# Head transposes in the last quarter of an expert's results, and a count of 48 ahead of two lists

## The chip, the cores and the metric

The kernel runs on one core of a Trainium2 chip. The metric is device time in microseconds (us), the median of several executions. A profiled execution is recorded beside them, with its own time. TensorE, the matmul engine, is called PE here; VectorE is DVE, ScalarE ACT, GpSimd POOL, and SyncE's DMA queue SP.

## What is computed

Three layers in a row on 2304 tokens (4 batches of 576, 8 heads of 64): an attention with a memory read, a feed-forward layer, and a mixture of eight experts. The edit lies in the third:

```python
logits = x @ w_gate
flat = logits.flatten()
order = np.argsort(-flat)
assigned = -np.ones(N, dtype=np.int64)
counts = np.zeros(E, dtype=np.int64)
for idx in order:
    tok, e = (int(idx) // E, int(idx) % E)
    if assigned[tok] >= 0 or counts[e] >= cap:
        continue
    assigned[tok] = e
    counts[e] += 1
...
for e in range(E):
    mask = assigned == e
    h = np.maximum(x[mask] @ w1[e], 0.0)
    out[mask] = h @ w2[e]
```

Here N = 2304, E = 8, cap = 288, the model width is 512 and the hidden width 1024. All values are float32.

## The kernel before

Each float32 operand of a large product is split into a high part (a copy on ACT, rounded to fp32r) and a low part (a subtraction on DVE or POOL); one product is three matmuls of the parts.

**Routing** (class `Moe`, generator `routes`). The assignment is made in phases. A phase finds the next expert that fills up: a search in two rounds of three steps (`search`), in which DVE compares (`cmp`), PE counts with 18 small products (line 727), DVE compares the counts with the room left (`fl`), and PE spreads the answer with one small product (line 732). Then come a count (line 779) and a prefix (lines 832 and 833). Behind it stand the expert's number, its four weight loads of 1 MB on SP (`load`), their conversion on ACT and POOL (`convert`, tiles `wraw` to `wsp`), and the list of its tokens (`lists`): DVE makes one-hot rows `oh` in two halves, PE multiplies them with 18 small products (line 870), DVE writes the indices `idx`, and POOL gathers 3 x 96 token rows into `xg` (`gather`, line 933). A list is made in small pieces beside the next expert's search: `spare` advances it where the search leaves room. `self.wants` says what the next piece needs: "v" DVE, "p" PE.

**Experts** (generator `mlps`). For each expert in the order found: 8 hidden blocks of 12 products (`hidden`, 288 columns each), then 4 result blocks of 24 products (`output`), each of 128 of the 512 result columns. The tokens of an expert come in by 12 transposes of `xg` into the PSUM tile `tr`, which has two buffers, and four splits into `xs` (`head`, pairs of k = 0, 1 and 2, 3). The results go out by 12 transposes (`tail`) in the next expert's hidden blocks 1 to 3, a copy on ACT and an indirect DMA on POOL.

**Order.** The order on PE is the program's: `mlps` yields after every product or transpose, and `run` counts these steps. The generator `routes` yields how many steps shall pass before its next small products are written; these numbers stand in `GAPS`, and GAPS[8] stands ahead of a list's product that no search accompanies:

```python
            for _ in self.mlps(routes):
                wait -= 1
                if wait <= 0 and len(self.ready) <= self.done + AHEAD:
                    wait = next(routes, NEVER)
```

While no list is ready, at the start, `run` takes the numbers only for a test (10 or more: write one piece of other work). A planner with a cost model of its own orders the instructions of DVE, ACT, POOL and SP within what the dependences allow. Weights are converted into six buffers, four for one expert; POOL runs its conversions, gathers and result transfers from one queue.

Before the change `mlps` wrote the first pair of the next expert's transposes ahead of result block 2, and the second pair ahead of block 3. In `routes`, list 6 (the last but one) was finished without any yield ahead of its product, and lists 0 and 7 with GAPS[8] = 36.

Of the kernel before, what the change touches and what calls it, by code (L numbers as in the profile page):

```python
# [359 lines left out]
KD = DM // 128  # L360
# [200 lines left out]
NE = 8  # L561
# [3 lines left out]
KE = FE // 128  # L565
# [5 lines left out]
CUTS = (2, 2, 2, 2)  # L571
ON_DVE = ()
LEAD = 12
HEAD_AT = 2
GAPS = (60, 12, 12, 15, 12, 12, 12, 18, 36, 6)
AHEAD = 3


class Moe:
# [127 lines left out]
    def search(self, val, hot, gaps, unit, beside=None):  # L707
# [3 lines left out]
        for s in range(3):  # L711
# [18 lines left out]
            pj = self.p1.tile([128, NE], F32, name="rs")  # L730
            yield GAPS[9]
            nc.tensor.matmul(pj, self.jones[unit][s][0:r], fl[0:r], start=True, stop=True)
# [9 lines left out]
    def phase(self):  # L742
# [24 lines left out]

        b = yield from self.search(hi, hot, GAPS[0:3], 0, lower)

        V.scalar_tensor_tensor(lw, hi, b, lof, op0=OP.subtract, op1=OP.add)  # L770
        b = yield from self.search(lw, hot, GAPS[3:6], 1)
        for s, op in enumerate((OP.is_gt, OP.is_equal)):
# [4 lines left out]
        ps = self.p1.tile([128, 2 * NTT * NE], F32, name="rs")  # L777
        yield GAPS[6]
        nc.tensor.matmul(ps, self.ones, gm.rearrange("p t e -> p (t e)"), start=True, stop=True)
# [47 lines left out]
    def prefix(self, ab):  # L827

        nc, V = self.nc, self.nc.vector
        pf = self.p1.tile([128, 2, 2, NTT], F32, name="rs")  # L830
        yield GAPS[7]
        nc.tensor.matmul(pf[:, 1], self.ones, ab[:, :, 0:NTT], start=True, stop=True)
# [50 lines left out]
    def routes(self):  # L883

        self.beside = self.wants = None
        for i in range(NE):
            if i < NE - 1:
                yield from self.phase()
            else:
                while self.wants is not None:  # L890
                    self.spare(self.wants)
                yield from self.rest()
            er = self.number()
            if i == 0:
                self.settle()
            self.split[i] = self.convert(self.load(er))
            self.beside = self.lists(i)
            self.wants = next(self.beside)
            if i in (0, NE - 1):
                while self.wants is not None:  # L900
                    if self.wants == "p":
                        yield GAPS[8]
                    self.spare(self.wants)

    def load(self, er):
        nc, raws = self.nc, []
# [86 lines left out]
    def mlps(self, routes):  # L993

        yield from self.head(0, range(KD))
        for i in range(NE):
            for f in range(KE):
                yield from self.hidden(i, f)
                if 1 <= f <= 3 and i:
                    yield from self.tail(i - 1, [f - 1])  # L1000
            for d in range(KD):
                if d >= HEAD_AT and i + 1 < NE and d < HEAD_AT + 2:
                    while len(self.ready) <= i + 1:
                        next(routes, None)
                    yield from self.head(i + 1, [2 * (d - HEAD_AT), 2 * (d - HEAD_AT) + 1])
                yield from self.output(i, d)
            self.done = i + 1
        yield from self.tail(NE - 1, range(3))

    def run(self, other, settle):  # L1010

        self.settle = settle
        with self.tc.manual_schedule(engines={mybir.EngineType.PE}):
            routes, wait = self.routes(), 0
            while not self.ready:
                if next(routes, 0) >= SLOW:
                    next(other, None)
            for _ in range(LEAD):
                wait = next(routes)
# [4 lines that stand above are left out]
# [106 lines left out]
```

## Time and profile before

| what | value |
|---|---|
| median of 3 runs (lowest to highest) | 1120.62 us (1119.87 to 1121.05) |
| profiled execution | 1114.29 us |
| its span, first to last instruction | 1112.6 us |
| what lies around the span | 1.69 us |
| mean granted TensorE clock | 0.933 |
| PE busy | 987.1 us (89%) |
| DVE, ACT, POOL busy | 663.3, 572.5, 533.9 us |

The profile is one execution, with times counted from the span's start. [...] The time in square brackets behind a row is the engine's idle time just before it, and what ended it. The expert stage starts near 796 us and PE's last product ends near 1105 us.

### The profile page before, as it was taken

To read this page: it belongs to the slowest core of one execution; us is meant where nothing else is said; L and a number is where in the kernel's file an instruction comes from. 1 tells how busy PE (TensorE), PEld (TensorE's weight loads), DVE (VectorE), ACT (ScalarE), POOL (GpSimd) and SP (SyncE) were. 2 spreads that over 40 slices of the span, in tenths; PEclk is the share of its full clock that TensorE was granted. 3 is DMA by queue.
4 is the path that set the end of the run, shared out by engine and by line. 5 is a ranking of instruction groups with operands and counts; after the bars stand their busy time and mean duration, and the time that the engine had idled before them with its cause. 6 is when DMAs were issued, how large, how long until landed. Compare 5 with 4: busy or idle time off the path is not lost.

```text
span 1112.6 us, 21194 instructions
## 1 busy us (share of the span) xinstructions
PE 987.1 (89%) x7561; PEld 907.2 (82%) x7561; DVE 663.3 (60%) x2012; ACT 572.5 (51%) x1471; POOL 533.9 (48%) x550
## 2 busy tenths in 40 slices
PE   4777799999999988999999999995679899969997
PEld 3555578888888978899999999983569888869996
DVE  7999887878788547783223232337756467653120
ACT  6877787978787645553223343421343244334531
POOL 3765656655566436553221112110772675575751
PEclk9877899999999999999999999995599899998998
DMA  6455435463444487475552323102453255425510
GB/s 147 113 138 135 124 109 167 103 176 92 141 97 132 135 294 249 131 232 197 202 162 95 114 86 102 52 19 55 161 174 135 60 195 172 137 83 192 174 37 29
DMA packets 135499, 148.74 MB, mean 134 GB/s; under 512 B 69857, under 2 KB 102625, under 8 KB 132321
## 3 DMA queue, kind: packets, MB, share of 16 engines
q1 hardware_dynamic: 132320, 137.94, 40.6%
q0 software_dynamic: 3072, 9.44, 2.8%
q8 instruction: 60, 0.98, 0.4%
q14 instruction: 47, 0.38, 0.1%
HBM read 109.60 MB, written 37.75 MB: 132 GB/s over the span
## 4 chain that ended last, share of the span: by engine, by line
PE 49%; DVE 21%; DMA 9%; issue 8%; ACT 7%; POOL 4%; SPq 1%; another core or an unknown queue 1%; POOLq 0%; DVEq 0%; ACTq 0%
PE ph L942 11%; PE ph L43 5%; PE ph L44 5%; PE ph L45 5%; PE py L43 3%; PE py L44 3%; PE py L45 3%; DMA raw<-in_moe_w_in_dram 3%; POOL wsp L925 2%; PE ps L308 2%; DMA wraw<-in_moe_w_dram 2%; PE rs L727 2%; PE ps L213 2%; DMA raw<-in_moe_w_out_dram 2%; DVE P L224 2%
## 5 line engine op out<-in xcount | busy, mean ns | idle before, releaser
L447 POOL TENSOR_TENSOR gf<-r 128x288 f32<-128x288 f32 x128 | 90.7, 709 | 239.2 <-ACT r L445 230.3
L925 POOL TENSOR_TENSOR wsp<-wraw,wsp 128x1024 fp32r<-128x1024 f32 x64 | 150.5, 2383 | 48.1 <-ACT wsp L923 45.4
L26 DVE TENSOR_TENSOR gs<-gf,gs 128x288 fp32r<-128x288 f32 x128 | 64.7, 506 | 106.5 <-ACT gs L25 106.1
L942 PE MATMUL ph<-xs,wsp 128*128 128x288 f32 x768 | 122.4, 310 | 0.0
L942 PE MATMUL ph<-hs,wsp 128*128 128x288 f32 x768 | 121.0, 313 | 0.0
L942 PEld LDWEIGHTS ph<-xs,wsp 128*128 128x128 f32 x768 | 109.1, 196 | 5.0 <-issue 4.3
L942 PEld LDWEIGHTS ph<-hs,wsp 128*128 128x128 f32 x768 | 110.6, 200 | 2.2 <-issue 1.4
L242 POOL TENSOR_SCALAR P<-P,R,og 128x128 f32<-128x128 f32 (+2 forms) x144 | 98.9, 703 | 23.2 <-DVE pta L26 9.6
L44 PE MATMUL py<-gs,wout 128*128 128x288 f32 x320 | 94.6, 298 | 0.9 <-DVE gs L26 0.8
L43 PE MATMUL ph<-xt,win 128*128 128x288 f32 x320 | 95.1, 297 | 0.1
L45 PE MATMUL ph<-xt,win 128*128 128x288 f32 x320 | 94.9, 297 | 0.0
L44 PE MATMUL ph<-xt,win 128*128 128x288 f32 x320 | 94.8, 296 | 0.0
L43 PE MATMUL py<-gs,wout 128*128 128x288 f32 x320 | 92.3, 298 | 1.6 <-ACT gs L25 1.1
L923 ACT ACTIVATE wsp<-wraw 128x1024 fp32r<-128x1024 f32 x64 | 63.9, 1050 | 57.7 <-DMA wraw<-in_moe_w_dram 36.8
L45 PE MATMUL py<-gs,wout 128*128 128x288 f32 x320 | 93.6, 296 | 0.0
L445 ACT ACTIVATE r<-ph 128x288 f32<-128x288 f32 x128 | 52.0, 406 | 76.6 <-PE ph L45 76.0
L236 ACT ACTIVATE P<-P,R 128x128 f32<-128x128 f32 (+2 forms) x144 | 83.4, 580 | 11.3 <-DVE R L224 10.8
L25 ACT ACTIVATE gs<-gf 128x288 fp32r<-128x288 f32 x128 | 56.5, 441 | 56.3 <-POOL gf L447 53.2
L213 PE MATMUL ps<-kt,qt 64*128 64x128 f32 (+3 forms) x384 | 58.7, 385 | 16.8 <-DVE ptb L26 9.1
L267 PE MATMUL ps<-ident,P 128*128 128x128 f32 x320 | 61.9, 302 | 11.5 <-DVE R L224 3.6
L43 PE MATMUL ph<-xs,win 128*128 128x288 f32 x192 | 62.8, 327 | 3.2 <-ACT yo L478 1.9
L26 DVE TENSOR_TENSOR ptb<-ps,ptb 128x384 fp32r<-128x384 f32 (+3 forms) x128 | 59.4, 466 | 8.8 <-ACT ptb L25 7.0
(227 smaller groups left out, 2683.8 us busy)
## 6 DMA issues: line engine op xcount, KB each, us to landing
wraw<-in_moe_w_dram SPq DMA_DIRECT2D x32, 1024.0 KB, 7.6
xt<-xs_d SPq DMA_DIRECT2D x16, 1152.0 KB, 5.7
x_d<-xo SPq DMA_DIRECT2D x32, 288.0 KB, 3.6
xf<-x_d SPq DMA_DIRECT2D x32, 288.0 KB, 3.5
xs_d<-xs SPq DMA_DIRECT2D x8, 1152.0 KB, 5.3
y<-yp_d SPq DMA_DIRECT2D x16, 576.0 KB, 5.4
raw<-in_moe_w_in_dram SPq DMA_DIRECT2D x32, 256.0 KB, 3.2
raw<-in_moe_w_out_dram SPq DMA_DIRECT2D x32, 256.0 KB, 2.9
```

Of the source, the lines that this page charges most:

```text
L26: (eng or nc.vector).tensor_tensor(lo, src, hi.bitcast(F32), op=OP.subtract)
L43: nc.tensor.matmul(out, lhi, rhi, start=start, stop=False)
L44: nc.tensor.matmul(out, lhi, rlo, start=False, stop=False)
L45: nc.tensor.matmul(out, llo, rhi, start=False, stop=stop)
L213: nc.tensor.matmul(ps[j][:, 0:w], qt[r0, a, qs], kt[r0, b, 0:w], start=i == 0, stop=i == 2)
L236: nc.scalar.activation(pw, pw, AF.Exp, bias=R[:, 0, u:u + 1], scale=-1.0, accum_out=R[:, 1, u:u + 1])
L242: nc.gpsimd.tensor_scalar(PP[n][w], PP[n][w], R[:, 2, w:w + 1], og9[:, hp, w:w + 1], op0=OP.mult, op1=OP.mult)
L267: nc.tensor.transpose(tr[:, 128 * i:128 * i + 128], P[:, 128 * i:128 * i + 128], ident)
L447: nc.gpsimd.tensor_tensor(gf, r, r, op=OP.mult)
L923: nc.scalar.activation(w[:, 0, hs], raw[:, hs], AF.Copy)
L925: eng.tensor_tensor(w[:, 1, hs], raw[:, hs], w[:, 0, hs].bitcast(F32), op=OP.subtract)
L942: nc.tensor.matmul(out, l[a], r[b], start=i + p == 0, stop=i == n - 1 and p == 2)
```

## The change

The first edit is in `mlps`. The next expert's transposes no longer stand ahead of result blocks 2 and 3. The blocks 0 to 2 are written whole; then come the first pair (k = 0 and 1), 12 products of block 3, the second pair (k = 2 and 3), and the other 12 products. The second is in `routes` and GAPS: finishing a list becomes a method, `finish`, which yields GAPS[8] ahead of the list's product. It is now used for list 6 as well, and GAPS[8] is 48 instead of 36.

```diff
-HEAD_AT = 2
-GAPS = (60, 12, 12, 15, 12, 12, 12, 18, 36, 6)
+GAPS = (60, 12, 12, 15, 12, 12, 12, 18, 48, 6)
...
             if i < NE - 1:
                 yield from self.phase()
             else:
-                while self.wants is not None:
-                    self.spare(self.wants)
+                yield from self.finish()
                 yield from self.rest()
...
             if i in (0, NE - 1):
-                while self.wants is not None:
-                    if self.wants == "p":
-                        yield GAPS[8]
-                    self.spare(self.wants)
+                yield from self.finish()
+
+    def finish(self):
+
+        while self.wants is not None:
+            if self.wants == "p":
+                yield GAPS[8]
+            self.spare(self.wants)
...
-            for d in range(KD):
-                if d >= HEAD_AT and i + 1 < NE and d < HEAD_AT + 2:
-                    while len(self.ready) <= i + 1:
-                        next(routes, None)
-                    yield from self.head(i + 1, [2 * (d - HEAD_AT), 2 * (d - HEAD_AT) + 1])
+            for d in range(KD - 1):
                 yield from self.output(i, d)
+            work = self.output(i, KD - 1)
+            if i + 1 < NE:
+                while len(self.ready) <= i + 1:
+                    next(routes, None)
+                for k in range(0, KD, 2):
+                    yield from self.head(i + 1, [k, k + 1])
+                    for _ in range(KE * 3 // 2 if k == 0 else 0):
+                        next(work)
+                        yield
+            yield from work
             self.done = i + 1
```

## Rows read from the trace of the kernel before

**Rows 1.** The page: busy time, share of the span and instructions of each engine.

```profile
PE 987.1 (89%) x7561; PEld 907.2 (82%) x7561; DVE 663.3 (60%) x2012; ACT 572.5 (51%) x1471; POOL 533.9 (48%) x550
```

**Rows 2.** Stretches: length, busy by engine (PE, PEld, DVE, ACT, POOL), PEclk, DMA, GB/s.

```profile
834.00:839.80 5.80, 5.80 (x39) 5.05 (x39) 1.67 (x6) 0.00 (x0) 1.06 (x1) 0.50 0.00 0
878.00:884.50 6.50, 6.50 (x30) 6.11 (x30) 3.59 (x16) 0.82 (x2) 2.00 (x1) 0.52 0.00 0
1019.00:1047.00 28.00, 28.00 (x216) 27.77 (x215) 5.30 (x12) 14.94 (x28) 22.69 (x12) 1.00 0.57 186
```

**Rows 3.** PE's timeline (start, us, instructions, idle before) at expert 1's head.

```profile
830.16 0.42 PE L954 MATMUL tr<-ident,xg 96*128 96x96 f32 x1 [4.08 <-DMA xg<-y_d,idx]
831.25 0.42 PE L954 MATMUL tr<-ident,xg 96*128 96x96 f32 x1 [0.67 <-DMA xg<-y_d,idx]
832.56 0.90 PE L954 MATMUL tr<-ident,xg 96*128 96x96 f32 x4 [0.88 <-DMA xg<-y_d,idx]
...
834.16 0.64 PE L727 MATMUL rs<-hot,cmp 128*32 128x8 bf16 x18
```

**Rows 4.** PE's timeline at expert 2's head.

```profile
873.76 0.61 PE L727 MATMUL rs<-hot,cmp 128*32 128x8 bf16 x18
875.08 0.30 PE L954 MATMUL tr<-ident,xg 96*128 96x96 f32 x1 [0.71 <-DMA xg<-y_d,idx]
877.14 1.34 PE L954 MATMUL tr<-ident,xg 96*128 96x96 f32 x5 [1.76 <-DMA xg<-y_d,idx]
```

**Rows 5.** PE's timeline from the last search to the prefix behind list 6.

```profile
986.18 0.16 PE L732 MATMUL rs<-fl,jo 32*128 32x8 bf16 x1 [3.14 <-DVE fl L729]
...
1001.33 1.85 PE L870 MATMUL rs<-rhs,oh 128*96 128x6 bf16 x18 [5.83 <-DVE oh L865]
1003.04 4.44 PE L942 MATMUL ph<-hs,wsp 128*128 128x288 f32 x18
1007.32 0.19 PE L832 MATMUL rs<-ab,ones 128*128 128x36 bf16 x1
```

**Rows 6.** POOL's timeline: conversions ahead of expert 1's gathers, and expert 7's last gather.

```profile
812.79 14.07 POOL L925 TENSOR_TENSOR wsp<-wraw,wsp 128x1024 fp32r<-128x1024 f32 x6 [10.07 <-ACT wsp L923]
...
829.46 0.92 POOL L933 DMA_INDIRECT xg<-y_d,idx  x1 [0.31 <-issue]
...
1019.00 0.92 POOL L933 DMA_INDIRECT xg<-y_d,idx  x1 [0.31 <-issue]
```

**Rows 7.** PE's timeline in late experts: one result block, a head pair, expert 7's head.

```profile
1040.52 3.45 PE L942 MATMUL ph<-hs,wsp 128*128 128x288 f32 x24
1043.81 0.66 PE L954 MATMUL tr<-ident,xg 96*128 96x96 f32 x6
...
1068.28 0.66 PE L954 MATMUL tr<-ident,xg 96*128 96x96 f32 x6
```

**Rows 8.** Instructions of the tile tr: ns min/median/max; PE's and PEld's waits for splits.

```profile
L25 ACT ACTIVATE xs<-tr x32: 404/411/421, 797.0 to 1072.8; 128x288 fp32r<-128x288 f32 x32
L26 DVE TENSOR_TENSOR xs<-tr,xs x32: 428/452/459, 797.5 to 1073.3; 128x288 fp32r<-128x288 f32 x32
...
DVE xs L26: 1.3, 2
```

**Rows 9.** DVE's timeline: reduction of the counts, flags, and list 6's one-hot rows.

```profile
843.46 0.47 DVE L781 TENSOR_REDUCE bank<-rs 128x16 f32<-128x288 f32 x1 [0.37 <-PE rs L779]
...
845.15 0.22 DVE L794 TENSOR_SCALAR ab<-bank,fm 128x18 bf16<-128x18 f32 x1
...
1000.23 2.01 DVE L865 TENSOR_TENSOR oh<-bank,slot 128x864 bf16<-128x864 f32 x2
```

**Rows 10.** ACT's timeline behind the second pair of expert 5's head.

```profile
1017.98 3.91 ACT L923 ACTIVATE wsp<-wraw 128x1024 fp32r<-128x1024 f32 x4 [1.14 <-issue]
```

**Rows 11.** ACT's waits from 796 to 1020 us: total, times, longest.

```profile
ACT wsp L923 <- DMA wraw<-in_moe_w_dram: 16.8, 10, 2.6
```

**Rows 12.** What PE waited for ahead of instructions of the tile rs: us, times.

```profile
DVE cmp L718: 14.0, 14
```

## Prediction

> **What bounds the kernel now.** I read the page's busy table first: TensorE (PE) is busy 89% of the span [rows 1]. A share over the whole kernel does not say which wait ends last in the stage that is edited, so I went next to the table by stretches for the expert stage. From 1019 to 1047 us PE is busy all 28 us at clock 1.00 and waits for nothing, while from 834.0 to 839.8 and from 878.0 to 884.5 it is busy at clock 0.50 and 0.52 [rows 2]. So the end of the stage is a full PE, and all that PE loses before 1019 us ends up in the total. Then I read PE's timeline for its idle times. Three places stand out: the transposes of expert 1's tokens (4.08 + 0.67 + 0.88 = 5.63 us of waiting for `xg`) [rows 3], those of expert 2 (0.71 + 1.76 = 2.47 us) [rows 4], and the product of list 6, which waits 5.83 us for its one-hot table `oh` [rows 5]. The first two belong to the first edit, the third to the second.
>
> Why is `xg` late? POOL has six weight conversions in front of expert 1's gathers, 14.07 us from 812.79, and issues the last of three gathers only at 829.46 [rows 6]; it lands 3.1 us later, when PE resumes at 832.56 [rows 3]. PE does not set these times, POOL's queue does.
>
> **The order of PE, counted.** PE's order is written out by the generators, so it can be counted from the code: each product or transpose is one step, and the routing generator is resumed after as many steps as it asked for. My count for the kernel before gives the order that the rows show (3 products after head 1's first six transposes, and then the 18 counting products of line 727) [rows 3]. For the changed code it says: the number of steps per expert is the same, no list is ever forced at the head (each is ready before), and the routing shifts against products and transposes by at most 12 steps, up to list 6.
>
> **Part 1, the heads one quarter later: expert 1.** 24 products now stand ahead of the first transposes. A row of 24 at full clock takes 1043.81 - 1040.52 = 3.29 us, 0.137 each [rows 7]. One counting group of 0.6 us comes ahead of the transposes too [rows 3]. Since the landing time is POOL's, PE does 3.9 us of work inside the old wait: 5.63 becomes 1.7. Gain 3.9.
>
> **Expert 2.** PE arrived there at 873.76 + 0.61 = 874.37; with 24 products more it arrives at 877.66, and the last landing was over at 877.14 [rows 4]. The wait of 2.47 goes, with 0.5 us to spare. If PE is earlier by then, POOL's chain ahead of these gathers is too: it starts with weights that are loaded once the routing has named the expert, and the routing is counted in PE's steps. Gain 2.47.
>
> **The clock behind both waits.** [...] Half the low time is lost: 5.8 / 2 = 2.9, and 6.5 x 0.48 = 3.1 us. Where expert 2's wait is gone I take all 3.1. At expert 1 a wait of 1.7 stays; 2.47 us of waiting brought the clock down at expert 2, and PE only transposes in between. Bounds 0 and 2.9; I take the middle, 1.45.
>
> **What the later heads cost.** Between the two pairs of transposes 12 products remain where 24 stood, and behind the second pair 12 where 24 stood. A pair's buffers (`tr`, two of them) are free after a copy of 0.41 us on ACT and a subtraction of 0.45 us on DVE for each [rows 8]. With both engines free that is some 1.8 us from the first transpose (an estimate: 0.33 for three transposes, 0.41, then the second copy beside the first subtraction, and the second subtraction, with the hand-overs between). The six transposes and 12 products take up to 0.66 + 12 x 0.137 = 2.3 us [rows 7]: hidden, with half a microsecond left. The cover is thin where the routing uses DVE. From the reduction of the counts (843.46) to the flags `ab` (845.37) DVE has 1.9 us of small steps, which PE covers with 18 steps, some 2.4 us [rows 7, 9]. Two subtractions in between (0.9 us) overrun that by 0.4, and with the hand-over of the counts from PE by 0.7. Bounds: 0, if the planner puts them elsewhere, and 0.9 at each of seven borders, 6.3. Routing runs beside four borders (0 to 1 up to 3 to 4); I take 0.7 at each, 2.8, since it is nearest to these DVE rows.
>
> Part 1: 3.9 + 2.47 + 3.1 + 1.45 - 2.8 = 8.1 us gained. Transposes, splits and transfers are the same in number; only their place on PE moves.
>
> **Part 2, 48 products ahead of list 6's product.** Before, the list's product follows the prefix directly, and PE waits 5.83 us [rows 5]: DVE still has the list to make, and its second half of `oh` ends at 1000.23 + 2.01 = 1002.24 [rows 9]. Behind the wait PE is slow: 18 products take 1007.32 - 1003.04 = 4.28 us where 18 x 0.137 = 2.47 is full clock, 1.8 lost, and the list's own 1003.04 - 1001.33 = 1.71 us shrinks in the same ratio to 1.0, 0.7 lost [rows 5]. The stall's price is 5.83 + 1.8 + 0.7 = 8.3 us. With the change 48 x 0.137 = 6.6 us of products stand there instead: PE reaches the list at 1002.1, when the first half of `oh`, which nine of its 18 products use, is a microsecond old, and the second all but done. DVE has nothing else in these products: they are results, which ACT copies out. What is left has the bounds 0 and 0.5; I take 0. Gain 8.3.
>
> Behind list 6 wait the naming of expert 7, its loads and its own list, now 48 + 12 steps later (60 x 0.137 = 8.2 us). Expert 7's last gather is issued at 1019.00 [rows 6] and the first transpose that reads one is at 1068.28 [rows 7]: some 48 us of cover. Cost 0. For expert 0 the number 36 or 48 only meets the test "10 or more": nothing changes.
>
> **Sum.** 8.1 + 8.3 = 16.4 us. The profiled execution takes 1114.29 us, 1.69 more than its span; by the sum it becomes 1097.9. The median of the runs is 1120.62, 6.3 above the profiled one; I carry the difference over, since the waits lie in the program's order: 1120.62 - 16.4 = 1104.2, say 1104.
>
> **The rivals.** *The borders give part 1 back.* A conversion on ACT lasts 1.0 us; four stand in one row right behind a second head pair, 3.91 us from 1017.98 [rows 10]. Heads a quarter later may find such conversions ahead. One at each of seven borders costs 7: 1111. For: `tr` has two buffers, and half a microsecond of cover. Against: conversions do not stand at every border.
>
> *Slower: splits behind conversions that themselves wait for weights.* ACT's conversions waited ten times for their loads, up to 2.6 us [rows 11]. A head split behind such a wait and two conversions comes 2.6 + 2.0 us late, of which 12 products hide 1.65: 2.95 us a border, 20.7 at seven, so 1104.2 + 20.7 = 1124.9. It decides from 16.4 / 7 = 2.3 us a border on. Against it: PE and its weight loads waited for a split only twice, 1.3 us in all [rows 8]. [...]
>
> *Nothing, because routing paces PE.* Were DVE's search the limit up to 995 us, and the list stall to come back elsewhere, the time would stay at 1120.6. Against: of 42 counting groups (seven phases of six) PE waited for DVE's comparison ahead of 14, 14.0 us in all, and some of that stands where no product can cover it [rows 12].
>
> *More.* DVE holds PE for 3.14 us at 986.18 [rows 5], a wait that no step of the change touches; if the new timing spares it and the borders cost nothing, 5.9 us more go: 1098.
>
> **How the numbers follow.** Forecast 0.52 (its own range 1097 to 1111: the clock term +-1.45, the borders -2.8 to +3.5, the stall of 986 gone or a second one); borders give it back 0.20; nothing 0.08; slower 0.15; more 0.05. So the likeliest is 1104. To leave out no more than 2 in 10 the range goes from 1097 to 1122. A difference of 0.2%, 2.2 us, is about what a measurement of this kernel can tell from none: faster 0.77, same 0.08, slower 0.15.
>
> **What would show it.** Right: PE's wait at expert 1's first transposes under 2 us, none at expert 2's, clock 1.00 behind the latter; no wait over 0.5 us at list 6 and clock 1.00 behind it; experts 5 to 7 as full as before, with the whole shift visible where they begin. Wrong: PE waits at `tr` for DVE or ACT between the two pairs, or at the first hidden products for `xs`; a new wait at line 727, 779 or 832 behind the splits; gathers issued later on POOL than before, since the planner orders POOL, ACT and DVE anew; the stall of 986 in another place, with the clock down behind it.

## The result, and the profile after

The changed kernel takes 1105.39 us in the median of 4 runs (1099.46 to 1109.36) against 1120.24 of the kernel before; the ratio is 0.9868, with a 95% interval of 0.9834 to 0.9902. That is 14.8 us less; forecast were 16.4 and a median of 1104. Its profiled execution took 1109.36 us with a span of 1107.6. Ratios here and below compare executions in the faster of two states only, which leaves out one execution, of 1520.56 us at a granted clock (PEclk in the views, a share of full speed) of 0.554, among the six of "pairs together".

A profile of 1109.36 against one of 1114.29 seems to say 4.9 us. The two executions differ ahead of the edit: the first head transpose starts at 803.92 us here, 7.7 later than the 796.26 of before, in a stretch whose order on PE is the same. One and the same kernel differs there by 4.5 and 5.6 us from profile to profile: this transpose starts at 796.26 and 800.76 in two profiles of the kernel before, and at 803.92, 799.29 and 798.34 in three of the changed one. So I compare the expert stage by itself, from the first head transpose to the last result transpose: 307.9 us before (796.26 to 1104.18), 295.3 after (803.92 to 1099.24), a gain of 12.6.

The lines that answer to [rows 3 to 5] and [rows 7], in PE's timeline of the kernel after (start, us, instructions, idle time before). Lines of the code are shifted by one or two: 869 is the list's product, 831 the prefix, 956 the head transposes.

```profile
837.77 0.28 PE L956 MATMUL tr<-ident,xg 96*128 96x96 f32 x1
838.77 0.30 PE L956 MATMUL tr<-ident,xg 96*128 96x96 f32 x1 [0.72 <-DMA xg<-y_d,idx]
840.14 0.30 PE L956 MATMUL tr<-ident,xg 96*128 96x96 f32 x1 [1.07 <-DMA xg<-y_d,idx]
...
883.70 0.66 PE L956 MATMUL tr<-ident,xg 96*128 96x96 f32 x6
884.14 1.04 PE L944 MATMUL ph<-hs,wsp 128*128 128x288 f32 x6
885.90 0.19 PE L831 MATMUL rs<-ab,ones 128*128 128x36 bf16 x1 [0.71 <-DVE ab L793]
...
988.34 0.16 PE L731 MATMUL rs<-fl,jo 32*128 32x8 bf16 x1 [3.07 <-DVE fl L728]
...
997.56 6.69 PE L944 MATMUL ph<-hs,wsp 128*128 128x288 f32 x48
1004.08 1.00 PE L869 MATMUL rs<-rhs,oh 128*96 128x6 bf16 x18
1004.94 2.63 PE L944 MATMUL ph<-hs,wsp 128*128 128x288 f32 x18
```

Expert 1's head waits 0.72 + 1.07 = 1.79 us where it waited 5.63; expert 2's does not wait; list 6's product comes without a wait behind 48 products, and the 18 products behind it take 2.63 us instead of 4.44. A new wait of 0.71 us stands at the prefix of expert 2's border. POOL's gathers are where they were with respect to its conversions. Counted from the running expert's first product, the last gather for expert 1 is issued after 30.4 us before and 30.3 after, and that for expert 2 after 29.1 and 29.5. So PE's later arrival, not an earlier transfer, is what removed the waits [rows 6]. For expert 1:

```profile
820.37 14.09 POOL L927 TENSOR_TENSOR wsp<-wraw,wsp 128x1024 fp32r<-128x1024 f32 x6 [10.02 <-ACT wsp L925]
834.60 0.92 POOL L935 DMA_INDIRECT xg<-y_d,idx  x1
...
837.06 0.92 POOL L935 DMA_INDIRECT xg<-y_d,idx  x1 [0.30 <-issue]
```

The table by stretches (columns as in [rows 2]) shows the clock: still 0.58 for 4.1 us behind expert 1's wait, 1.00 behind list 6, and, not foreseen, 0.57 over 8 us in the middle of expert 1, far from any head (behind a wait of 0.89 us in the search).

```profile
840.90:845.00 4.10, 4.10 (x25) 3.78 (x22) 2.09 (x8) 0.41 (x1) 1.77 (x1) 0.58 0.00 0
868.00:876.00 8.00, 8.00 (x63) 7.25 (x62) 1.93 (x8) 2.54 (x4) 7.57 (x5) 0.57 0.17 54
...
1004.00:1008.00 4.00, 4.00 (x44) 3.92 (x44) 2.10 (x11) 0.30 (x1) 1.87 (x2) 1.00 1.03 393
...
1042.42:1070.75 28.33, 28.33 (x219) 27.97 (x218) 6.13 (x14) 14.02 (x28) 21.01 (x11) 1.00 0.20 59
```

Expert 5 is not quite as full as before. Here a result product waits for a hidden copy that stands behind two conversions on ACT (2.00 us from 1028.57 on; the copy starts at 1030.47). PE's timeline:

```profile
1030.92 7.41 PE L944 MATMUL ph<-hs,wsp 128*128 128x288 f32 x51 [0.62 <-ACT hs L967]
```

For the runs that follow I use one table: the time from an expert's first hidden product to the next expert's, in us, from PE's timeline of each profile (the last column is the stage as defined above; expert 7 takes 28.5 to 28.7 in all).

| kernel | e0 | e1 | e2 | e3 | e4 | e5 | e6 | stage |
|---|---|---|---|---|---|---|---|---|
| before | 46.2 | 43.0 | 39.1 | 43.1 | 48.8 | 28.2 | 28.2 | 307.9 |
| before, second profile | 46.7 | 41.6 | 38.9 | 45.5 | 48.7 | 28.2 | 28.2 | 309.2 |
| changed | 40.1 | 42.1 | 39.9 | 43.5 | 39.9 | 30.2 | 28.3 | 295.3 |
| changed, second | 41.2 | 39.7 | 39.2 | 40.2 | 35.4 | 29.2 | 28.3 | 284.6 |
| changed, third | 41.4 | 39.6 | 39.0 | 38.6 | 35.5 | 29.3 | 28.4 | 283.0 |
| heads only | 41.1 | 39.5 | 39.4 | 38.9 | 45.7 | 28.3 | 28.3 | 292.6 |
| list only | 46.0 | 41.6 | 38.1 | 39.2 | 35.2 | 29.0 | 28.2 | 288.6 |
| 24 instead of 48 | 41.5 | 39.9 | 39.3 | 40.3 | 42.6 | 28.4 | 28.3 | 291.6 |
| one conversion on DVE | 41.7 | 38.8 | 39.8 | 41.6 | 38.1 | 30.1 | 28.4 | 289.8 |
| pairs together | 42.0 | 38.0 | 40.1 | 43.3 | 43.1 | 30.2 | 29.3 | 297.4 |
| head 1 later | 36.1 | 40.9 | 39.3 | 40.9 | 39.8 | 30.1 | 28.3 | 286.9 |
| head 1 later, again | 37.0 | 39.8 | 39.5 | 38.6 | 35.5 | 29.2 | 28.3 | 279.2 |
| all heads later | 36.9 | 38.6 | 45.0 | 39.3 | 36.5 | 32.9 | 29.5 | 290.3 |
| heads 1 and 2 later | 36.1 | 40.3 | 45.0 | 38.4 | 35.5 | 29.2 | 28.3 | 284.1 |

The table needs one reading rule. In the last search (expert 4) PE waited 2.6 to 3.2 us for DVE's `fl`, but not in every profile: in both first profiles, in the second one of before and in the three that were measured on the same chip as it ("one conversion", "pairs together", "head 1 later"), and in none of the other eight, from two further chips. (On which chip the first two profiles were taken is not recorded.) Columns e3 to e5 are compared only within one of these two groups.

### The profile page after: what moved, and what is told of

Its sections match the earlier page's. It is cut to its first block, busy times and chain, and to the rows that moved or that the text cites. A ratio compares the mean times of both kernels' runs of the same rounds, so it can differ in the third digit from the quotient of the medians.

```text
span 1107.6 us, 21191 instructions
## 1 busy us (share of the span) xinstructions
PE 992.2 (90%) x7561; PEld 913.0 (82%) x7561; DVE 661.3 (60%) x2012; ACT 572.2 (52%) x1471; POOL 533.1 (48%) x550
## 4 chain that ended last, share of the span: by engine, by line
PE 55%; DVE 18%; issue 7%; ACT 7%; DMA 7%; POOL 3%; SPq 2%; another core or an unknown queue 0%; POOLq 0%; DVEq 0%; ACTq 0%
PE ph L944 13%; PE ph L43 6%; PE ph L44 5%; PE ph L45 5%; PE py L43 3%; PE py L44 3%; PE py L45 3%; PE ps L308 3%; PE rs L726 2%; DMA raw<-in_moe_w_out_dram 2%; PE ps L213 2%; ACT P L236 2%; DMA wraw<-in_moe_w_dram 2%; DMA raw<-in_moe_w_in_dram 2%; DVE qpt L196 2%
## 5 line engine op out<-in xcount | busy, mean ns | idle before, releaser
L242 POOL TENSOR_SCALAR P<-P,R,og 128x128 f32<-128x128 f32 (+2 forms) x144 | 97.6, 692 | 27.8 <-DVE pta L26 11.9
L944 PEld LDWEIGHTS ph<-hs,wsp 128*128 128x128 f32 x768 | 108.0, 195 | 2.9 <-issue 1.1
L224 DVE CUSTOM_DVE_ANT_0 P<-ps,maskw 128x128 f32<-128x128 f32 (+3 forms) x128 | 59.4, 484 | 11.4 <-PE ps L213 6.9
```

Source lines behind the costliest of these rows:

```text
L242: nc.gpsimd.tensor_scalar(PP[n][w], PP[n][w], R[:, 2, w:w + 1], og9[:, hp, w:w + 1], op0=OP.mult, op1=OP.mult)
L944: nc.tensor.matmul(out, l[a], r[b], start=i + p == 0, stop=i == n - 1 and p == 2)
```

## The experiments

**Heads only.** The whole edit of `mlps`, without `finish` for list 6 and with 36 for the count:

```diff
-GAPS = (60, 12, 12, 15, 12, 12, 12, 18, 48, 6)
+GAPS = (60, 12, 12, 15, 12, 12, 12, 18, 36, 6)
...
-                yield from self.finish()
+                while self.wants is not None:
+                    self.spare(self.wants)
                 yield from self.rest()
```

> Part 1 alone: the heads stand in the last result block, and list 6 is finished as in the kernel before, with no products ahead of it (GAPS[8] = 36). My theory, two gains that add up: the expert stage (first head transpose to last result transpose) loses the waits of experts 1 and 2 and some slow clock, and is shorter than the 307.9 us of before by 12.6 - 8.5 = 4 us (what the profile of the change shows) to 8.1 us (the prediction's sum); list 6 still waits about 5.8 us; ratio to the kernel before 0.993 to 0.997. Rival, that the moved heads bring nothing because the borders give it all back: stage as before within 1 us, and a ratio of 1.000.

Measured: ratio 0.9928 (0.9902 to 0.9955), 8.0 us of the 1111.6 that the kernel before takes on that chip. Expert 0 takes 41.1 us. List 6 waits to the hundredth as before, and the clock behind it is 0.50 for 7.4 us (PE's timeline, then stretches):

```profile
993.59 1.84 PE L869 MATMUL rs<-rhs,oh 128*96 128x6 bf16 x18 [5.83 <-DVE oh L864]
```

```profile
993.60:1001.00 7.40, 7.31 (x43) 7.08 (x44) 3.06 (x15) 0.00 (x0) 2.79 (x3) 0.50 0.99 370
```

The heads gain by themselves; that the borders give all back is refuted. The stage that I had forecast, 4 to 8.1 us under 307.9, cannot be read off: this profile is without the stall of the last search, and no profile of the kernel before is.

**List only.** The heads of before; ahead of `rest` the list is finished with a yield, and the count is 48:

```diff
                 while self.wants is not None:
+                    if self.wants == "p":
+                        yield GAPS[8]
                     self.spare(self.wants)
                 yield from self.rest()
```

> Part 2 alone: the heads stand ahead of result blocks 2 and 3 as before, and 48 products stand ahead of list 6's product (and 48 instead of 36 ahead of list 7's). My theory: expert 4 alone is shorter, by 8.3 to 8.9 us, all else in the stage as before, ratio 0.992 to 0.993. Rival, that the wait comes back elsewhere: a new wait of several us between list 6 and expert 6, ratio above 0.997.

Measured: ratio 0.9903 (0.9873 to 0.9933), 10.8 us. Expert 4 takes 35.2 us, 10.5 less than in the heads-only run where I had put 8.3 to 8.9; no wait of more than 0.9 us stands behind it, and expert 0 keeps its 46.0. The two parts add to 18.8 us alone (each +-3); together, on that chip, they gave 13.2 (ratio 0.9881, 0.9853 to 0.9909). The 5.6 us between are about what the three intervals allow; whether the parts take something from each other stays open. In the stages the second part is worth 292.6 - 284.6 = 8.0 beside the first, and the first 288.6 - 284.6 = 4.0 beside the second (9.6 and 5.6 with the changed kernel's third profile, of another chip).

**24 instead of 48.**

```diff
-GAPS = (60, 12, 12, 15, 12, 12, 12, 18, 48, 6)
+GAPS = (60, 12, 12, 15, 12, 12, 12, 18, 24, 6)
```

> The whole change, but with 24 products ahead of list 6's and list 7's products instead of 48. My theory (the list's one-hot rows are done at a time that PE does not set, so products fill the wait one for one): 24 products fill 3.3 of 5.8 us, a wait of about 2.5 us stays at list 6 and some slow clock behind it; expert 4 is 2.5 to 4.5 us longer than with 48. Rival, that any products in between make the one-hot rows later by as much: a wait near 5 us.

Measured: ratio 0.9931 (0.9907 to 0.9955). The wait is 2.51 us, the time that 24 products leave of 5.83:

```profile
993.22 1.85 PE L869 MATMUL rs<-rhs,oh 128*96 128x6 bf16 x18 [2.51 <-DVE oh L864]
```

```profile
993.00:1001.00 8.00, 7.69 (x48) 7.46 (x49) 3.59 (x18) 0.41 (x1) 2.79 (x3) 0.58 1.00 364
```

The mechanism holds one for one. My price did not: expert 4 is 42.6 - 35.4 = 7.2 us longer, not 2.5 to 4.5. Of these 0.9 is list 7's product, which stands in expert 4 here and in expert 5 with 48. The clock behind the shorter wait is 0.58 over 8 us, 3.4 us lost, nearly what the 5.83 us wait cost (7.4 x 0.50 = 3.7). Filling half a wait saved half the wait and next to nothing of the clock.

**The changed kernel again**, unedited, twice:

> The changed kernel once more, nothing edited. It tells what of the profile of the change repeats. If the slow clock of 869 to 876 us in expert 1 (clock 0.57 over 8 us, behind a wait of 0.9 us) belongs to the change, expert 1 takes about 42.1 us again; if it fell there by chance, expert 1 takes 38 to 39.5 us, as the prediction's sum says (43.0 - 2.5 - 3.1 + 0.7 = 38.1). The waits of 1.8 us at expert 1's head and about 3.1 us in the last search should repeat either way. Ratio to the kernel before about 0.987.

> The changed kernel again, unedited, on the same chip as the three that follow, so that their ratios can be set beside its own (0.987 and 0.988 so far). Expert 0 takes 40 to 41.5 us, with 1.7 us of waiting for the gathers.

Measured: 0.9881 (0.9853 to 0.9909) and 0.9863 (0.9835 to 0.9891). Expert 1 takes 39.7 and 39.6 us: the 42.1 of the first profile was the top of a spread, but the sum's 38.1 is not reached either. A part of the slow clock repeats, behind the same wait (PE's timeline and a stretch, second profile): 12 products take 2.96 us where the 12 at 868.30 take 1.86, and 10 us at clock 0.83 lose 1.7.

```profile
861.63 0.16 PE L731 MATMUL rs<-fl,jo 32*128 32x8 bf16 x1 [0.69 <-DVE fl L728]
...
863.65 2.96 PE L944 MATMUL ph<-hs,wsp 128*128 128x288 f32 x12
```

```profile
858.00:868.00 10.00, 9.04 (x93) 8.49 (x91) 5.35 (x15) 6.98 (x9) 10.00 (x6) 0.83 0.56 190
```

That wait is older than the change (0.52 us at 863.43 in the kernel before, with clock 1.00 from 863 to 868 and 12 products in 1.75 us behind it). The 3 us in the last search did not repeat.

**The kernel before again**, unedited:

> The kernel before once more, nothing edited, for a second profile of it. If the gains seen in the stage are the program's, its waits repeat: 5.6 us at expert 1's head, 2.3 to 2.5 at expert 2's, 5.8 at list 6, and the stage takes 300 to 308 us against 284.6 of the changed kernel's second profile. The 3.1 us in the last search stood in the first profiles of both kernels and in none of the four since: my theory is that it is not of the program, and it may be there or not; the rival, that the moved heads or the 48 products spare it, wants it here again.

Measured in one execution: 1120.06 us, a stage of 309.2. List 6 waits 5.83 us again, expert 1's head 4.07 + 0.62 + 1.00 = 5.7, expert 2's 2.1. The stall of the last search is here (PE's timeline):

```profile
992.07 0.16 PE L732 MATMUL rs<-fl,jo 32*128 32x8 bf16 x1 [3.15 <-DVE fl L729]
...
1007.34 1.85 PE L870 MATMUL rs<-rhs,oh 128*96 128x6 bf16 x18 [5.83 <-DVE oh L865]
```

In the profiles kept it comes and goes with the chip and not with the kernel: it falls in with neither the change nor its absence.

**One conversion on DVE.** Of expert 1's first weight part, the second half's subtraction goes to DVE:

```diff
-            self.split[i] = self.convert(self.load(er))
+            self.split[i] = self.convert(self.load(er), ((0, 1),) if i == 1 else ON_DVE)
...
-                eng = nc.vector if (len(wh), h) in ON_DVE else nc.gpsimd
+                eng = nc.vector if (len(wh), h) in on_dve else nc.gpsimd
```

> The changed kernel with one of the eight weight conversions' subtractions of expert 1 on DVE instead of POOL, so that POOL has five ahead of the gathers instead of six. My theory: POOL's queue sets what is left of the wait at expert 1's head; the gathers come about 2.4 us earlier, the 1.7 us of waiting go, and with them some of the slow clock behind (expert 0 takes 1.7 to 3.5 us less than the 41.2 of the changed kernel, less about 1 us if the conversion delays DVE's search). Rival, that the gathers wait for the list's indices or the transfer: wait as before.

Measured: ratio 0.9882 (0.9853 to 0.9910). The first three lines are POOL's timeline, the next is DVE's, the others are PE's:

```profile
816.05 2.39 POOL L927 TENSOR_TENSOR wsp<-wraw,wsp 128x1024 fp32r<-128x1024 f32 x1 [9.69 <-ACT wsp L925]
818.76 14.65 POOL L927 TENSOR_TENSOR wsp<-wraw,wsp 128x1024 fp32r<-128x1024 f32 x6 [0.32 <-ACT wsp L925]
833.56 0.92 POOL L935 DMA_INDIRECT xg<-y_d,idx  x1
```

```profile
816.95 2.57 DVE L927 TENSOR_TENSOR wsp<-wraw,wsp 128x1024 fp32r<-128x1024 f32 x1 [0.47 <-ACT wsp L925]
```

```profile
820.67 0.81 PE L726 MATMUL rs<-hot,cmp 128*32 128x8 bf16 x18 [2.71 <-DVE cmp L717]
837.82 0.30 PE L956 MATMUL tr<-ident,xg 96*128 96x96 f32 x1 [0.39 <-DMA xg<-y_d,idx]
839.09 0.30 PE L956 MATMUL tr<-ident,xg 96*128 96x96 f32 x1 [0.97 <-DMA xg<-y_d,idx]
```

The run is not the test that I meant. POOL has 1 + 6 conversions ahead of the gathers here, not five: the planner put all seven that are left there, and the first gather is issued 833.56 - 802.76 = 30.8 us after expert 0's first product, against 834.60 - 806.76 = 27.8 in the first profile of the changed kernel. The conversion takes 2.57 us on DVE, not the one that I had put, and the search behind it makes PE wait 2.71 us. (A conversion on POOL runs beside it until 818.44, and DVE ends 1.08 us later; whether DVE alone would be faster was not tested.) The head's wait falls from 1.8 to 0.39 + 0.97 = 1.36 us because PE comes later (first transpose 837.18 - 802.76 = 34.4 us after expert 0's first product, against 837.77 - 806.76 = 31.0), and the clock is 1.00 from 834 to 846. Expert 0 is no shorter (41.7). What the rows do show is what the gathers stand behind: PE's product for the list ends at 827.71 + 0.93 = 828.64, POOL converts until 833.41, and the first gather follows at 833.56. The kernel before has the same order with DVE's write of `idx` beside it: 822.68, conversions until 826.86, first gather at 827.00. So it is POOL's queue and not the list; what an earlier gather would be worth stays open.

**Pairs together.** The 12 products between the pairs are left out of that place; the whole of block 3 follows the 12 transposes:

```diff
                 for k in range(0, KD, 2):
                     yield from self.head(i + 1, [k, k + 1])
-                    for _ in range(KE * 3 // 2 if k == 0 else 0):
-                        next(work)
-                        yield
             yield from work
```

> The changed kernel without the 12 products between the two pairs: all 12 transposes, then the whole of result block 3. My theory: the two tr buffers are free only some 1.8 us after the first transpose, so PE now waits about 1.1 to 1.5 us for a split at each of seven borders, 8 to 10 us in all, and the ratio to the kernel before rises by 0.006 to 0.009 over the changed kernel's. Rival, that the 12 products cover nothing since the splits are not what is waited for: no wait at tr, and the time of the changed kernel within 2 us.

Measured: ratio 0.9899 (0.9870 to 0.9927). In PE's timeline a wait for DVE's split stands at all seven borders, 0.80 us at five, 1.19 at one, and 0.31 at expert 1's, where the gathers are waited for first; two of them:

```profile
1005.96 0.91 PE L956 MATMUL tr<-ident,xg 96*128 96x96 f32 x6 [0.80 <-DVE xs L26]
...
1036.21 0.83 PE L956 MATMUL tr<-ident,xg 96*128 96x96 f32 x6 [0.80 <-DVE xs L26]
```

Sum 5.5 us, against 8 to 10 expected, and the ratio lies 0.002 to 0.004 above the changed kernel's three, not 0.006 to 0.009 (the changed kernel was not run on this chip): a buffer comes free sooner than I had put (0.80 us of waiting, not 1.1 to 1.5). So the 12 products cover a wait that is there without them, and 0.80 of their 1.65 us is needed: about 0.8 us are left as cover, not 0.5.

**Expert 1's head later.** Only at the first border, 12 products stand ahead of each pair, and none between the second pair and expert 1's first products:

```diff
                 for k in range(0, KD, 2):
+                    for _ in range(KE * 3 // 2 if i == 0 else 0):
+                        next(work)
+                        yield
                     yield from self.head(i + 1, [k, k + 1])
-                    for _ in range(KE * 3 // 2 if k == 0 else 0):
+                    for _ in range(KE * 3 // 2 if k == 0 and i else 0):
                         next(work)
                         yield
```

> The changed kernel with only expert 1's head later by 12 products more: the first pair in the middle of result block 3, the second at its end. My theory: 12 products fill 1.65 of the 1.7 us that are left of the wait, but behind the second pair stand only six hidden products (0.8 us) ahead of the first that needs k = 2, while its split takes about 1.3 us and DVE has the routing's small steps: of the 1.7 us about 1 is won, and the clock stays up behind it (another 1 to 2 us). Expert 0 and 1 together 1 to 3 us less than the 80.9 of the changed kernel. Rival, that the splits' lateness takes all: no less.

> Expert 1's head later by 12 products more, once more (0.982 before, on another chip than the changed kernel). My theory: the clock behind expert 1's wait is worth more than the wait; expert 0 takes about 36 us against 40 to 41.5, expert 1 about 1 us more, and the ratio lies 0.003 to 0.005 below the changed kernel's on this chip. Rival, that the lower ratio was the chip's: equal within 0.002.

Measured: 0.9823 (0.9797 to 0.9849) and, beside the changed kernel's 0.9863 on one chip, 0.9816 (0.9791 to 0.9841): 1089.58 us against 1095.51 and 1110.82, the fastest version here. Stretches behind expert 1's wait, first of the changed kernel (third profile), then of this one:

```profile
832.00:836.00 4.00, 2.17 (x27) 1.67 (x26) 0.52 (x2) 0.82 (x2) 3.98 (x3) 0.85 0.25 81
836.00:841.50 5.50, 5.50 (x26) 5.17 (x26) 2.89 (x11) 1.23 (x3) 0.97 (x1) 0.50 0.00 0
```

```profile
832.00:836.00 4.00, 4.00 (x46) 3.63 (x45) 1.78 (x8) 0.57 (x2) 3.83 (x3) 1.00 0.38 107
836.00:841.50 5.50, 4.39 (x37) 4.08 (x36) 4.76 (x23) 1.68 (x6) 1.82 (x1) 1.00 0.01 3
```

Filling the last 1.8 us of waiting shortens expert 0 by 41.4 - 37.0 = 4.4 us: the clock at 0.50 over 5.5 us was the larger part. That is more than I had put at first: experts 0 and 1 together take 77.0 and 76.8 us, 3.9 and 4.1 less than 80.9, not 1 to 3. A wait of 1.11 us for DVE comes back at the prefix at 839.84, behind both pairs of transposes (835.39 and 837.64); DVE is busy 4.76 of the 5.5 us there, and the clock stays at 1.00.

**All heads later**, and **heads 1 and 2 later**: the same edit with the test true for every border, or `i < 2`.

> All seven heads later by 12 products: first pair in the middle of result block 3, second pair at its end. My theory: the cover of the second pair's splits is then the six hidden products ahead of k = 2 (0.8 us) against about 1.3 us from the pair's first transpose to the first split of it, so PE waits 0.2 to 0.6 us at each border, and experts 5 and 6, which have no routing beside them, take 28.5 to 28.9 us instead of 28.3; the ratio is that of expert 1's head alone or up to 0.003 above it. Rival, a border that costs nothing: experts 5 and 6 as before, and the same ratio; or one that costs over 1 us: experts 5 and 6 above 29.4.

> Only the heads of experts 1 and 2 later by 12 products. At expert 2's border the first pair now stands behind the prefix at line 831, so that its splits are no longer between the counts and the flags on DVE. My theory: the 0.7 us of waiting at line 831 there go, and 0.2 to 0.6 come back at the hidden products; expert 1 takes 0 to 0.7 us less than with expert 1's head alone. Rival, that the 0.7 us are not the splits' doing: the wait at line 831 stays.

Measured: 0.9909 (0.9876 to 0.9941) and 0.9853 (0.9830 to 0.9877). At the border from expert 4 to 5, where no search runs, PE waits twice (all heads later), and again so at the next; experts 5 and 6 take 32.9 and 29.5 us, beyond the 0.2 to 0.6 us that I had put. The ratio is 0.009 above that of expert 1's head alone, where I had allowed 0.003:

```profile
1000.55 0.83 PE L956 MATMUL tr<-ident,xg 96*128 96x96 f32 x6 [0.83 <-DVE xs L26]
...
1002.85 1.02 PE L944 MATMUL ph<-xs,wsp 128*128 128x288 f32 x3 [0.65 <-ACT xs L25]
```

With two heads later the wait at line 831 of expert 2's border is gone, as the theory had it: the first split starts at 881.80 there, behind the flags `ab` at 880.16, where in the changed kernel two splits (884.65 and 885.10, 0.9 us) stand ahead of them (885.47). That wait was the splits'. Expert 1 is still no shorter than with expert 1's head alone (40.3 against 39.8). And expert 2 takes 45.0 us instead of 39.0, in both kernels. Its profile (ACT's, DVE's and PE's timelines, then stretches, of the kernel with two):

```profile
898.55 2.01 ACT L925 ACTIVATE wsp<-wraw 128x1024 fp32r<-128x1024 f32 x2 [1.34 <-DMA wraw<-in_moe_w_dram]
```

```profile
901.37 0.46 DVE L968 SCALAR_TENSOR_TENSOR hs<-ph,hs 128x288 fp32r<-128x288 f32 x1 [1.80 <-ACT hs L967]
901.74 0.16 DVE L735 CUSTOM_DVE_ANT_0 sc<-rs,nb 128x8 f32<-128x8 f32 x1
```

```profile
901.96 1.53 PE L869 MATMUL rs<-rhs,oh 128*96 128x6 bf16 x18 [1.88 <-DVE nb L735]
```

```profile
904.00:908.00 4.00, 4.00 (x29) 3.72 (x29) 0.56 (x2) 0.41 (x1) 4.00 (x2) 0.50 0.01 4
908.00:912.00 4.00, 4.00 (x22) 3.69 (x21) 1.55 (x6) 0.41 (x1) 2.93 (x4) 0.50 0.33 96
```

ACT waits 1.34 us for weights, then converts for 2.0; the hidden block's copy stands behind it. DVE's `hs` waits for that copy, and behind `hs` stands the search's `sc`, which reads the tile `rs`; that tile has one buffer, and PE's list product writes it next. PE waits 1.88 us, and the clock is 0.50 for 8 us. This is the slower rival's mechanism, with the hidden copies in place of the splits, in a kernel where it decides. In these rows ACT's copy starts at 900.94, behind a result copy and the conversions that end at 900.56, and DVE's `sc`, whose `rs` PE had written by 900.07, starts at 901.74, behind the `hs` that waited 1.80 us; more than these rows no run shows of it. With all heads later the list's product of expert 2 waits 0.68 us and a search ahead of it 1.38, and 15 products behind take 3.95 us as here; ACT and DVE were not read there. Why the timing of expert 2's weights and copies meets so badly in these two kernels and not in the others was not settled.

## Why the prediction was right, point by point

The time and the mechanism of both parts were right: PE's waits at the two heads and at list 6 shrank by the products put ahead of them. The terms are not all the size that I gave them, and that the sum came near is in part luck.

- **Expert 1's wait** (gain 3.9, 1.7 left): 1.79, 1.67 and 1.83 us left in the three profiles. Right.
- **The clock behind it** (gain 1.45, half of 2.9): right in the first profile only, where 4.1 us at 0.58 lose 1.7. In the third, 3.4 us are lost between 832 and 846 (mostly the 5.5 us at 0.50), against 3.9 in the list-only run, which has the heads of before (0.70 over 13 us behind the wait): some 0.5 gained. Expert 0 still fell by 4.6 to 4.8 us between these runs (46.0 against 41.4 and 41.2), where the sum had 3.9 + 1.45 - 0.7 = 4.65. That agreement is luck: the border's 0.7 did not come there either.
- **Expert 2's wait** (gain 2.47): gone in every run with the change.
- **The clock behind expert 2's wait** (3.1): the term that was mis-sized; nothing of it came. Over the whole of expert 1 the granted clock is as low with the change as without. The slow stretch only changed its place, from behind expert 2's wait (in the list-only run 10 us at clock 0.83, 1.7 us) to behind a wait of 0.6 to 0.9 us in the search (1.7 us in the second profile, 3.4 in the first). Expert 1 gained about 1.9 us (41.6, 41.6 and 43.0 against 39.6, 39.7 and 42.1), not 4.9: the wait less the 0.71 us at the border. I had taken the clock's loss from one execution and supposed that nothing else would bring it down. The stretches show expert 1 in two profiles of before, then in two of the changed kernel:

```profile
845.30:888.30 43.00, 39.14 (x356) 36.03 (x355) 26.31 (x106) 15.73 (x27) 24.35 (x14) 0.92 0.38 126
850.30:891.90 41.60, 37.82 (x355) 34.70 (x354) 26.40 (x107) 15.71 (x27) 24.33 (x14) 0.96 0.39 131
```

```profile
846.84:888.95 42.11, 39.15 (x356) 35.88 (x354) 26.84 (x109) 15.62 (x27) 24.35 (x14) 0.92 0.37 129
843.30:883.00 39.70, 37.57 (x355) 34.82 (x354) 26.35 (x106) 15.68 (x27) 24.37 (x14) 0.96 0.41 137
```

- **The borders** (cost 2.8): 0.71 us at expert 2's border in every profile of the change, up to 0.22 at expert 1's, and 0.16 at expert 6's (28.33 against 28.17). That the 0.71 is the splits standing between counts and flags on DVE was shown by moving them (heads 1 and 2 later, where PE does not wait at the prefix at 880.80). The size is the 0.7 that I had put for a border, but at one border and not at four. Sum of what was found: about 1.1, two fifths of the term, inside its bounds. Away from the borders the changed kernel waits 0.96 to 1.17 us for a list's reduction in expert 2; one of the three profiles with the old heads has such a wait too (0.94), so whether the edit brings it is open.
- **List 6** (gain 8.3): 45.7 - 35.4 = 10.3 us in expert 4, of which 0.9 is list 7's product moved to expert 5: 9.4. The wait of 5.83 was exact; the slow clock behind it was 3.7 us here where I had 2.5. Behind it nothing came back in the repeats; in the first profile 0.62 us did, in expert 5. Expert 7's list, 60 steps later, cost nothing (expert 7 takes 28.5 us before and after).
- **The sum**: 16.4 forecast, 14.8, 13.2 and 15.2 us by the three ratios (the last two 1111.6 x 0.0119 and 1110.8 x 0.0137). By the stages part 2 is worth 8.0 to 9.6 us (8.3 forecast) and part 1 only 4.0 to 5.6 beside it (8.1 forecast): 4.55 us of clock were put in where some 0.5 came, and the borders, put 1.7 too dear, met a part of that.
- **The rivals**: that borders give part 1 back, and that nothing changes, fell with the heads-only and list-only runs. The stall of the last search, which "more" rested on, is not the program's. The slower one did not decide in this kernel; a neighbour of it (heads 1 and 2 later) shows that its mechanism can, by way of the hidden copies.

The 7.7 us by which the first 800 us differ between the first two profiles are of the size by which one kernel differs from itself there (4.5 and 5.6 us); what makes that spread was not found.

## What to carry to other kernels

A wait of PE can have two prices, the wait and the slow clock behind it, and in these runs the second hardly shrank with the first (3.7 us behind 5.83, 3.4 behind 2.51): work that filled half a wait earned half a wait, work that filled the last 1.8 us earned the clock as well (0.50 over 5.5 us became 1.00). And a gain of clock at one place was lost at another (in expert 1, 1.7 to 3.1 us behind the wait at expert 2's head without the change, 1.7 to 3.4 behind a search's wait with it), so read the clock over the whole stage, in more than one profile. So fill a wait wholly at the place that has it (here one border), and leave the other places alone: the same shift at every border used up the cover of the splits in the late experts and cost more than it won (6.0 us of the cost stand in expert 2, where the kernel with two heads shows the chain on ACT and DVE told above). When one stage of a long program is edited, compare that stage between the profiles, since the rest can differ by as much as the gain.

## What the hardware showed beyond that

- The clock's loss did not follow the wait's length: 3.7 us behind 5.83 us of waiting, 3.4 behind 2.51, 2.7 (5.5 us at 0.50) behind 1.83, 1.7 behind 0.69, none behind 1.11 nor behind 1.36 (one conversion on DVE). In the search beside expert 1 a wait of 0.5 to 0.9 us stands in all fourteen profiles; behind it 12 products take 2.25 to 3.02 us in seven of them and 1.75 to 1.77 in the other seven (granted clock where it was read: 0.57 over 8 us, 0.83 over 10 and 0.72 over 6 in the changed kernel's three, 1.00 over 5 in the kernel before). What decides it was not found.
- In six of the fourteen profiles PE waited 2.58 to 3.15 us for DVE's `fl` in the last search. In the three of them whose DVE timeline was read (both of the kernel before, the first of the changed one) DVE stood still for 4.69 to 4.79 us ahead of it; the profile names no engine for it, and POOL issued gathers and result transfers meanwhile (981.36 to 984.76 in the first profile of before). In the other eight PE does not wait there (DVE's gap is 1.02 us in the changed kernel's second profile), and on their two chips the kernel before took 1111 us instead of 1119 and 1120. What DVE waits for was not found.
- Within one kernel on one chip the time spreads by several us (1091.32 to 1098.91 for the changed kernel's third run); the per-expert times repeat to a few tenths where no wait differs.
